# Attention values with queries on the partitions, and f32 loads cast on GpSimd, in a fused sliding-window attention and gated-convolution FFN

## The chip, the core and the metric

The kernel runs on one core of a Trainium2 chip. The metric is the device time of one execution in microseconds (us), the median of several runs. Runs of one kernel agree within 1.5% here.

Engine names as the profile writes them: PE is TensorE (matmuls), PEld its weight load, DVE is VectorE, ACT is ScalarE, POOL is GpSimd, SP is SyncE (here only an issuer of transfers). "SPq" and "POOLq" are their sequencers. A line number such as L237 is a line of that kernel's own file, so the same statement has different numbers in different kernels.

## The reference, cut to what matters

```python
def _attn_ref(q, k, v):                     # q, k, v: (8, 8, 576, 64) f32
    scores = np.matmul(q, k.transpose(0, 1, 3, 2)) / np.sqrt(64)
    mask = np.abs(pos[:, None] - pos[None, :]) <= 32      # sliding window, symmetric
    scores = np.where(mask, scores, -1e9)
    attn = np.exp(scores - scores.max(-1, keepdims=True))
    attn = attn / (attn.sum(-1, keepdims=True) + 1e-09)
    return np.matmul(attn, v)

def _moe_ref(x, w_in, conv_w, w_out):       # x: (8, 576, 512), w_in: 512x1024, w_out: 1024x512
    h = np.maximum(x @ w_in, 0.0)
    conv_out = sum(conv_w[k] * shifted(h, k) for k in range(3))   # along the sequence
    gate = 1.0 / (1.0 + np.exp(-conv_out))
    return h * gate @ w_out                 # f32, (8, 576, 512)
```

Eight batches go through attention (eight heads, handled as four pairs) and then through the FFN. All matmuls of the kernels read bf16 and write f32 tiles.

## The kernel before

Each batch's q, k and v are loaded by transfers that GpSimd issues. They cast f32 to bf16 on the way. A row of one head is 256 bytes in HBM, so every transfer is made of 256-byte pieces. The loads of batch 0 are issued head by head (32 issues), those of later batches block by block:

```python
    def load_qk(b, per_head):
        i = b % NLD
        for (dst, src) in ((qnb_pp[i], q), (knb_pp[i], k)):
            if not per_head:
                _load_rows(nc, nc.gpsimd, dst, src, b, 0, H, S)        # 5 transfers, all heads
        if per_head:
            for h in range(H):
                _load_rows(nc, nc.gpsimd, qnb_pp[i], q, b, h, 1, S)    # 2 transfers for one head
                _load_rows(nc, nc.gpsimd, knb_pp[i], k, b, h, 1, S)
    # ... load_v: blocks of v on gpsimd into ve; then vo, the same rows shifted by 64, copied from ve:
        nc.sync.dma_start(vo[0:64, :, :, :], ve[64:128, 0:NBLK - 1, :, :])
        nc.sync.dma_start(vo[64:128, :, :, :], ve[0:64, 1:NBLK, :, :])
```

GpSimd also makes the diagonal matrices of the convolution weights, in its queue ahead of the loads of batch 1, and VectorE scales w_out by 0.5 once it has landed:

```python
    def load_weights():
        # ... w_in on gpsimd, conv_w on sync
        for kk in range(3):
            for m in range(MB):
                nc.gpsimd.tensor_scalar(
                    out=diag_w[:, kk, m, :], in0=ident,
                    scalar1=conv_w_sb[:, kk, m:m + 1], scalar2=None, op0=ALU.mult,
                )
    def load_w_out():
        nc.gpsimd.dma_start(w_out_sb, moe_w_out.rearrange("(c p) f -> p c f", p=128))
        nc.vector.tensor_scalar(out=w_out_sb, in0=w_out_sb, scalar1=0.5, ..., op0=ALU.mult)
```

Attention for a pair of heads: q and k are transposed on TensorE, the scores come out key-major (keys on the partitions), are exponentiated and masked, and then the values are computed **transposed** (head dimension on the partitions, queries along the free axis), which is the form the FFN wants. The sums of the softmax come from a matmul with a matrix of ones, so each sum is repeated on 64 partitions, and the reciprocal is taken of all 128x576 copies:

```python
    def job_av(g):
        # ...
        for t in range(NT):
            for e in range(2):
                nc.tensor.matmul(flat(po)[64*e:64*e+64, 64*t:64*t+64], vt[:, 2*pr+e, :],
                                 attn[:, e, 64*t:64*t+64], start=True, stop=True)
        for (x0, x1) in ((0, 512), (512, S)):
            for e in range(2):
                nc.tensor.matmul(flat(pd)[64*e:64*e+64, x0:x1], ones, attn[:, e, x0:x1],
                                 start=True, stop=True)
        rec = apool.tile([128, S], FP32, name="rec", tag="rec")
        nc.vector.reciprocal(rec, flat(pd)[:, 0:S])
        nc.vector.tensor_tensor(out=xT[b][:, pr, :], in0=flat(po)[:, 0:S], in1=rec, op=ALU.mult)
```

The FFN's jobs (`job_ph`: w_in and ReLU; `job_pc`: convolution, tanh and gate; `job_py`: w_out and store) of one batch are interleaved with the attention jobs of the next.

The softmax here doesn't subtract the row's maximum and nothing guards it: scores larger than these inputs give would overflow.

## Time and profile before

| | before |
|---|---|
| time, median | 348.03 us (347.66 to 349.21), 3 runs |
| profiled span | 345.0 us |
| start, until the last `xT` of batch 0 is written | 73.9 us |
| seven periods, one batch each | 237.8 us, 34.0 each |
| tail (last FFN alone) | 33.3 us |

The page of the profile, cut: busy time by engine; the span in 40 slices of 8.6 us (a digit is the busy tenths; PEclk is the clock granted to TensorE in tenths); the chain of waits that ended last, by engine and by line.

```profile
PE 254.0 (74%) x2766; PEld 166.1 (48%) x2784; DVE 232.4 (67%) x215; ACT 155.9 (45%) x245; POOL 137.8 (40%) x187
...
PE   0024106558889888988898889998898889988995
...
POOL 8999999659350805080408140632200000000000
PEclk9999555559999999999999998999999999999999
...
PE 42%; DVE 25%; POOL 16%; ACT 10%; DMA 4%; issue 2%; POOLq 0%
...
L237 DVE RECIPROCAL rec<-ps 128x576 f32<-128x576 f32 x32 | 120.2, 3755 | 24.8 <-PE ps L228 24.8
```

No engine is full on average, and the chain is shared: that is the picture of engines that wait for one another in turn. The last line says that 32 reciprocals took 3,755 ns each, 120 us in all, half of all that VectorE did. The slices say where PE is empty or slack: the first nine, in which POOL is mostly full. In slices 5 to 9 the granted clock is about half. The runs speak against the clock as a cause of the long time: runs of this kernel with a mean granted clock of 0.92 or 0.93 took 346.7 to 350.4 us, those with 0.97 to 0.99 took 345.6 to 349.8.

How the start is spent shows in the chain in order of time (start us, duration us, what):

```profile
22.59 0.18 POOL ident masks.py:197
...
31.31 14.64 POOL diag_w L148 x24
45.96 4.26 POOL qnb_74 L28 x5
...
58.97 12.94 DMA w_out_sb<-in_moe_w_out_dram
71.92 1.23 DVE w_out_sb L155
73.15 0.68 DVE xT L238
73.87 3.28 PE ps L249 x13
```

Until 22.6 us POOL issues loads, and only then makes `ident`, which PE's first transpose waits for. POOL makes `diag_w` until 46 us, and only then issues the q and k of batch 1. Then the chain runs through the load of w_out and its scaling, which stands ahead of the last `xT` in VectorE's program. Three FFN matmuls (L249) already ran at 64.9 us and the others had to wait for that `xT`; from 73.9 us the FFN runs on.

The busy time by stretch, for the start, the seven periods and the tail (columns: from:to, length, then busy us and count of instructions for PE, PEld, DVE, ACT and POOL, then the granted clock, DMA share and GB/s):

```profile
0.00:73.90 73.90, 18.83 (x270) 13.52 (x271) 30.01 (x43) 12.93 (x20) 66.31 (x100) 0.73 1.14 99
73.90:311.70 237.80, 206.12 (x2322) 135.37 (x2337) 195.69 (x165) 128.03 (x204) 71.46 (x88) 0.98 0.83 87
```

In the periods PE is busy 87% and VectorE 82%; neither is full.

### The profile page before, as it was taken

The numbers are of one execution on the slowest core, as the hardware profiler recorded it, in microseconds if no ns is written. First come the engines' busy times: TensorE is split into PE (matmuls) and PEld (weight loads), VectorE is DVE, ScalarE is ACT, GpSimd is POOL, SyncE is SP. The second block draws the span as 40 slices with busy tenths as digits, with TensorE's granted clock in tenths as the row PEclk, the third lists the DMA queues.
The fourth block names the chain that finished last, engine by engine and source line by source line (L and its number), as shares of the span: only waits on it lengthen the run. The fifth ranks groups of instructions, "written<-read, shape, count | busy, mean of one in ns | idle before, by whom it ended". The sixth has DMA issues, their size and how long they took to land.

```text
span 345.0 us, 6548 instructions
## 1 busy us (share of the span) xinstructions
PE 254.0 (74%) x2766; PEld 166.1 (48%) x2784; DVE 232.4 (67%) x215; ACT 155.9 (45%) x245; POOL 137.8 (40%) x187
## 2 busy tenths in 40 slices
PE   0024106558889888988898889998898889988995
PEld 0024103336655655565556555655555655555652
DVE  3018333939997869787878696878786978793130
ACT  1015002225654645465546454556554655443552
POOL 8999999659350805080408140632200000000000
PEclk9999555559999999999999998999999999999999
DMA  8869689999948994999499939691911001100114
GB/s 41 54 43 118 136 55 132 169 162 135 145 31 101 128 132 30 104 123 137 58 103 117 145 25 107 90 171 38 120 68 63 2 2 61 61 33 2 62 63 153
DMA packets 123934, 30.33 MB, mean 88 GB/s; under 512 B 116736, under 2 KB 117760, under 8 KB 123904
## 3 DMA queue, kind: packets, MB, share of 16 engines
q0 software_dynamic: 114608, 16.26, 70.4%
q1 hardware_dynamic: 9296, 13.65, 12.7%
q8 instruction: 22, 0.36, 0.4%
q14 instruction: 8, 0.07, 0.1%
HBM read 32.52 MB, written 9.44 MB: 122 GB/s over the span
## 4 chain that ended last, share of the span: by engine, by line
PE 42%; DVE 25%; POOL 16%; ACT 10%; DMA 4%; issue 2%; POOLq 0%
DVE rec L237 17%; PE ps L290 16%; PE ps L249 13%; PE ps L266 9%; POOL diag_w L148 4%; DMA w_out_sb<-in_moe_w_out_dram 4%; ACT y_sb L297 3%; DVE gT L276 3%; ACT attn L205 2%; DVE xT L238 2%; POOL qnb_73 L20 2%; POOL knb_75 L20 2%; ACT tn L273 2%; DVE attn L206 2%; PE ps L220 2%
## 5 line engine op out<-in xcount | busy, mean ns | idle before, releaser
L237 DVE RECIPROCAL rec<-ps 128x576 f32<-128x576 f32 x32 | 120.2, 3755 | 24.8 <-PE ps L228 24.8
L249 PE MATMUL ps<-xT,w_in_sb 128*128 128x288 bf16 x512 | 77.3, 293 | 20.8 <-DVE xT L238 11.4
L249 PEld LDWEIGHTS <-w_in_sb 128*128 128x128 bf16 x512 | 50.4, 99 | 38.7 <-issue 24.8
L290 PE MATMUL ps<-w_out_sb,gT 128*128 128x512 bf16 x270 | 64.3, 379 | 2.0 <-ACT tn L273 0.6
L273 ACT ACTIVATE tn<-ps 128x576 f32<-128x576 f32 x64 | 41.8, 653 | 25.1 <-PE ps L266 23.5
L266 PEld LDWEIGHTS <-diag_w 128*128 128x128 bf16 x384 | 35.0, 97 | 20.2 <-issue 11.4
L205 ACT ACTIVATE attn<-ps 128x576 bf16<-128x576 f32 x64 | 38.6, 652 | 11.2 <-PE ps L196 11.2
L290 PEld LDWEIGHTS <-gT 128*128 128x128 bf16 x288 | 27.7, 98 | 32.7 <-issue 2.2
L297 ACT COPY y_sb<-ps 128x1024 f32<-128x1024 f32 (+1 forms) x20 | 18.5, 927 | 53.2 <-PE ps L290 53.2
L185 ACT CAST qT<-ps 128x576 bf16<-128x576 f32 x32 | 20.4, 636 | 47.6 <-PE ps L176 47.6
L206 DVE TENSOR_TENSOR attn<-attn,mask 128x1152 bf16<-128x1152 bf16 x32 | 24.0, 750 | 22.4 <-ACT attn L205 22.4
L276 DVE SCALAR_TENSOR_TENSOR gT<-tn,hT_85 128x576 bf16<-128x576 f32 x32 | 23.6, 738 | 15.6 <-ACT tn L273 15.2
L255 ACT ACTIVATE hT_84<-ps 128x576 bf16<-128x576 f32 x32 | 20.9, 655 | 25.9 <-PE ps L249 25.5
L104 POOL DMA_DIRECT2D ve_78<-in_v_dram x24 | 18.9, 830 | 33.6 <-PE ps L220 33.6
L266 PE MATMUL ps<-hT_85,diag_w 128*128 128x288 bf16 x192 | 28.5, 286 | 3.1 <-ACT hT_85 L255 2.9
L255 ACT ACTIVATE hT_85<-ps 128x576 bf16<-128x576 f32 x32 | 20.8, 654 | 22.0 <-PE ps L249 21.8
L266 PE MATMUL ps<-hT_84,diag_w 128*128 128x288 bf16 x192 | 28.7, 288 | 2.4 <-ACT hT_84 L255 2.4
L104 POOL DMA_DIRECT2D ve_77<-in_v_dram x24 | 19.0, 831 | 23.6 <-PE ps L220 22.5
L238 DVE TENSOR_TENSOR xT<-ps,rec 128x576 bf16<-128x576 f32 x32 | 23.9, 747 | 5.9 <-PE ps L220 5.8
L28 POOL DMA_DIRECT2D qnb_74<-in_q_dram x20 | 16.9, 864 | 20.5 <-PE ps L176 20.3
L176 PE MATMUL ps<-ident,qnb_73 128*128 128x128 bf16 (+1 forms) x80 | 7.3, 228 | 24.1 <-POOL ident masks.py:199 23.9
L276 DVE SCALAR_TENSOR_TENSOR gT<-tn,hT_84 128x576 bf16<-128x576 f32 x32 | 23.2, 731 | 2.5 <-ACT tn L273 2.5
(68 smaller groups left out, 276.2 us busy)
## 6 DMA issues: line engine op xcount, KB each, us to landing
out_dram<-y_sb SPq DMA_DIRECT2D x16, 512.0 KB, 3.3
vo_79<-ve_77 SPq DMA_DIRECT2D x8, 256.0 KB, 4.7
qnb_74<-in_q_dram POOLq DMA_DIRECT2D x16, 128.0 KB, 5.9
knb_76<-in_k_dram POOLq DMA_DIRECT2D x16, 128.0 KB, 6.2
vo_80<-ve_78 SPq DMA_DIRECT2D x8, 256.0 KB, 4.1
ve_77<-in_v_dram POOLq DMA_DIRECT2D x12, 128.0 KB, 4.5
ve_78<-in_v_dram POOLq DMA_DIRECT2D x12, 128.0 KB, 4.3
qnb_73<-in_q_dram POOLq DMA_DIRECT2D x12, 128.0 KB, 7.4
```

Source lines behind the costliest of these rows:

```text
L104: nc.gpsimd.dma_start(ve[d0:d0 + s1 - s0, c, :, :], v[b, :, s0:s1, :].rearrange("h p d -> p h d"),)
L205: nc.scalar.activation(attn[:, e, :], flat(pss[e])[:, 0:S], AF.Exp, bias=0.0, scale=scale)
L206: nc.vector.tensor_tensor(out=attn, in0=attn, in1=mask.rearrange("p t x -> p (t x)")[:, None, :].broadcast_to([128, 2, S]), op=ALU.mult,)
L237: nc.vector.reciprocal(rec, flat(pd)[:, 0:S])
L238: nc.vector.tensor_tensor(out=xT[b][:, pr, :], in0=flat(po)[:, 0:S], in1=rec, op=ALU.mult)
L249: nc.tensor.matmul(ps[:, gg, 0:TG], w_in_sb[:, kc, m * 128:(m + 1) * 128], xT[b][:, kc, gg * TG:(gg + 1) * TG], start=(kc == 0), stop=(kc ...
L255: nc.scalar.activation(hT[:, m, 1:S + 1].rearrange("p (gg x) -> p gg x", x=TG), ps[:, :, 0:TG], AF.Relu)
L266: nc.tensor.matmul(ps[:, gg, 0:TG], diag_w[:, kk, m, :], hT[:, m, gg * TG + kk:gg * TG + kk + TG], start=(kk == 0), stop=(kk == 2),)
L273: nc.scalar.activation(tn.rearrange("p (gg x) -> p gg x", x=TG), ps[:, :, 0:TG], AF.Tanh, bias=0.0, scale=0.5)
L276: nc.vector.scalar_tensor_tensor(out=gT[b // 2][:, m, b % 2, :], in0=tn, scalar=1.0, in1=hT[:, m, 1:S + 1], op0=ALU.add, op1=ALU.mult,)
L290: nc.tensor.matmul(ps[:, i, :], g_[:, m, 128 * tb:128 * tb + 128], w_out_sb[:, m, :], start=(m == 0), stop=(m == MB - 1),)
L297: nc.scalar.copy(out=y_sb[:, 0:n, :], in_=ps[:, 0:n, :])
```

## The change

Its intent is in two halves.

**The attention half.** The value matmuls get attention as the stationary operand and v, with a 65th column of ones, as the moving one. So the result is query-major: queries on the partitions, and the softmax sum as one more column. The reciprocal is taken of 128x10 sums instead of 128x576. The price: the result must be transposed on TensorE (`job_xt`) and copied from PSUM by VectorE.

**The load half.** q, k and v are loaded as f32, without a cast, on SyncE's queue (the profile lists it as "hardware_dynamic"; here: the hardware queue) into staging tiles; GpSimd casts them (23 casts of 512 columns a batch). `vo` is cast from the staging tile instead of copied by a transfer. The loads and casts are spread between the jobs. Batch 0 is loaded in 15 blocks. `ident` comes early, `diag_w` moves from GpSimd to VectorE, and the scaling of w_out disappears (the 0.5 goes into the ReLU).

The core of the diff (cuts marked `# ...`; the load order, the merge of the streams and the moved memsets are left out):

```diff
-    ve_pp = [pp.tile([128, NBLK, H, 64], BF16, name=f"ve{i}") for i in range(NLD)]
+    qst = pp.tile([128, NBLK, H, 64], FP32, name="qst")      # kst, vst alike
+    ve_pp = [pp.tile([128, NBLK, H, 65], BF16, name=f"ve{i}") for i in range(NLD)]
 # ...
+    def load_block(dst, src, b, c, lo):
+        s0, s1 = max(0, lo), min(S, lo + 128)
+        fixed(nc.sync.dma_start(
+            dst[s0 - lo:s1 - lo, c, :, :], src[b, :, s0:s1, :].rearrange("h p d -> p h d")))
+    def cast(out_, in_):
+        fixed(nc.gpsimd.tensor_scalar(
+            out=out_, in0=in_, scalar1=1.0, scalar2=0.0, op0=ALU.mult, op1=ALU.add))
 # ...
+    for t_ in ve_pp + vo_pp:
+        nc.vector.memset(t_[:, :, :, 64], 1.0)
 # ...  diag_w
-                nc.gpsimd.tensor_scalar(
+            nc.vector.tensor_scalar(
 # ...  load_w_out
-        nc.vector.tensor_scalar(
-            out=w_out_sb, in0=w_out_sb, scalar1=0.5, scalar2=None, op0=ALU.mult
-        )
 # ...  job_av
+        for c in range(NBLK):
             for e in range(2):
-                nc.tensor.matmul(
-                    flat(pd)[64 * e:64 * e + 64, x0:x1],
-                    ones,
-                    attn[:, e, x0:x1],
-                    start=True, stop=True,
-                )
+                for j in range(2):
+                    t = min(2 * c + j, NT - 1)
+                    nc.tensor.matmul(
+                        pf[64 * j:64 * j + 64, AVS * c + 65 * e:AVS * c + 65 * e + 65],
+                        attn[:, e, 64 * t:64 * t + 64],
+                        (ve if t % 2 == 0 else vo)[:, t // 2, 2 * pr + e, :],
+                        start=True, stop=True,
+                    )
-        rec = apool.tile([128, S], FP32, name="rec", tag="rec")
-        nc.vector.reciprocal(rec, flat(pd)[:, 0:S])
+        rec = apool.tile([128, NBLK, 2], FP32, name="rec", tag="rec")
+        nc.vector.reciprocal(rec, po[:, :, :, 64])
         nc.vector.tensor_tensor(
-            out=xT[b][:, pr, :], in0=flat(po)[:, 0:S], in1=rec, op=ALU.mult
+            out=xn[b][:, :, 2 * pr:2 * pr + 2, :], in0=po[:, :, :, 0:64],
+            in1=rec[:, :, :, None].broadcast_to([128, NBLK, 2, 64]), op=ALU.mult,
         )
+    def job_xt(g):
+        t_ = transpose_into(slot(), lambda c: xn[b][:, c, 2 * pr:2 * pr + 2, :]...)
+        nc.vector.tensor_copy(out=xT[b][:, pr, :], in_=t_)
 # ...  job_ph
+            bias=0.0, scale=0.5,
```

## The prediction

> **What bounds it now.** Span 345.0 us; PE is busy 74%, DVE 67% (busy table). The chain of waits is shared: PE 42%, DVE 25%, POOL 16%; its largest line is the reciprocal `rec` on DVE (17%). There are three stages.
>
> 1. Start, 0 to about 74 us. In the timeline, POOL issues 32 small loads until 22.3 us, so `ident` is late and PE starts at 23.85. Then POOL makes `diag_w` (31.2 to 46 us), so the loads of batch 1 start at 45.9 and PE waits for them at 49 to 55. DVE then sits on the `w_out_sb` scaling until 73.1, behind a load that took 12.9 us. The steady FFN begins at 73.9 us, at half clock until 80.
> 2. Seven periods of one batch each. The same `xT` copy on the chain recurs at 138.0, 172.9, 207.4, 243.8, 278.3 us: about 35 us a period. Summed from start-to-start times of the timeline, PE needs about 27 us a period. DVE needs 30 (four reciprocals of 3.76 us are 15 of it). Neither is full; they alternate.
> 3. Tail, about 312 to 345 us: PE alone, dense.
>
> **What the change does.**
> - DVE: a pair's reciprocal goes from 128x576 (3.76 us) to 128x10 (estimate 0.15-0.2). The multiply goes from 576 to 640 columns (0.75 to about 0.8), and a 128x576 PSUM copy (0.75, as `kT`) is added. That is 4.5 to about 1.8 us a pair, about 88 us in all: busy 232 to about 150, 19 us a period, no longer limiting.
> - PE: the `ones` matmuls go (about 1.1 us a period), and four sets of transposes come (0.3 us each); the AV matmuls take about as long. Still 27 to 28 us a period.
> - Loads: 1024 rows of 256 B each on the hardware queue, in f32, with no POOL issue (0.83-0.92 us each) and no `vo` transfers. The old queue moved about 1,000 to 1,200 rows/us; the hardware queue moved the 4-byte pieces of `conv_w` at over 1,300/us. A batch's 13,824 rows take 10 to 14 us, which does not limit.
> - POOL: 23 casts of 512 columns per batch. `diag_w` (128 columns) came every 0.58 us; I estimate 0.9 to 1.15 us for 512, so 21 to 26 us a period. [...] the two `diag_w` that met the mask multiply came after 1.12 and 0.85 us instead of 0.58. Twelve such DVE instructions a period (mask, `gT`) cost POOL up to 6 us more. So POOL lands at 27 to 32 us, level with PE: the new rival.
>
> **Time.** Start: q and k in by about 13 us, PE from about 15, first AV about 20, FFN from about 41 instead of 74: gain about 32 us. Periods: 35 to about 31 us, with PE above 85% busy: gain about 27 us. Tail unchanged. 348 - 59 = about **289 us**; 8 in 10 between 272 and 312. Faster by over 2%: 0.94; within 2%: 0.04; slower: 0.02.
>
> **What would show it.** PE's first matmul near 15 us; FFN matmuls from about 41 us; recurrence of `xT` at 29-32 us; DVE share near 50%; `rec` gone from the chain, which becomes mostly PE; casts at 0.9-1.15 us, some stretched to 1.5+ beside mask and `gT`.
>
> **What would make it wrong.** Casts above 1.3 us, or long blocking: POOL then sets the period (34 us or more, about 320 us), with PE transposes waiting for casts. [...] If PE packs as in the tail, 275.

Three statements are cut out of the recorded text, because no trace or run of this case shows what they said: a general statement on contention between VectorE and GpSimd (what was measured of it here stands near the end), one on loads behind stores, one on the lowest rate at which the start would hold. No term of the sum goes with them: 348 - 32 - 27 = 289 us, as recorded. Three terms were estimates, which the trace before did not show: the 0.15 to 0.2 us of the short reciprocal; what 384 more columns add to a GpSimd instruction, from the 0.58 us of `diag_w` to 0.9 to 1.15; and the contention, which extends two delays in that trace (1.12 and 0.85 us instead of 0.58, so 0.54 and 0.27 more) to twelve instructions a period, `gT`'s among them, whose effect it had not seen. The two rates are in the trace before: GpSimd issued the 4,608 rows of one q in 4.26 us, about 1,080 rows/us, and the 3,072 pieces of `conv_w` took 2.31 us from the first to the last, about 1,330 a us.

## More of the kernel before

The attention stream is ahead by two pairs: before the values of a batch's last pair, the program has the transposes of the first two pairs of the **next** batch.

PE's longest wait in total, after that for `ident` at the start, is the FFN's wait for values that VectorE has not delivered (total us, times, longest us):

```profile
PE ps L249 <- DVE xT L238: 11.4, 11, 3.5
```

## The result, and the profile after

| | before | after |
|---|---|---|
| time, median of the same rounds | 348.62 us (347.66 to 350.84) | 284.78 us (284.04 to 285.84) |
| ratio after/before | | 0.8164 (95%: 0.8114 to 0.8213) |
| profiled span | 345.0 us | 282.3 us |
| start | 73.9 us | 44.5 us |
| seven periods | 237.8 us (34.0 each) | 204.4 us (29.2 each) |
| tail | 33.3 us | 33.4 us |

Four runs of each. A ratio is the mean time of one kernel's runs over that of the other's of the same rounds, so it is not quite the ratio of the medians. The stages are cut, to about 0.1 us, at the end of the last `xT` copy of batch 0 and of batch 7. The gain is 29.4 us in the start and 33.4 us in the periods, together the 62.7 us by which the spans differ, to rounding.

The page of the changed kernel's profile, the same lines (slices of 7.1 us):

```profile
PE 247.8 (88%) x2880; PEld 169.4 (60%) x2880; DVE 164.0 (58%) x269; ACT 159.3 (56%) x253; POOL 130.4 (46%) x189
...
PE   0356649987899999999999999999999999999994
...
POOL 4583579996788358244756273736353000000000
PEclk9999999999999999999999999999999999999999
...
PE 75%; DMA 8%; ACT 7%; SPq 4%; DVE 2%; issue 1%; POOL 1%; ACTq 0%
```

The chain is now TensorE's: 75%, with VectorE down from 25% to 2% and GpSimd from 16% to 1%. PE is full from slice 12 on. By stretch:

```profile
0.00:44.50 44.50, 21.08 (x257) 14.54 (x258) 23.52 (x68) 16.36 (x26) 25.52 (x45) 1.00 1.22 194
44.50:248.90 204.40, 197.19 (x2442) 137.27 (x2442) 133.04 (x193) 127.35 (x206) 104.91 (x145) 1.00 0.71 143
```

In the periods PE is busy 96% of the time (28.2 of 29.2 us). Before it was 206.1 of 237.8. So of the 33.4 us that the periods lost, 24.5 us is PE's waiting and 8.9 us its busy time. The latter is not fewer matmuls: the run below that only shortens the reciprocal has all the matmuls of before, and from the first FFN matmul of batch 1 to that of batch 7 PE is busy 170.9 us in it, against 181.3 before and 171.8 after. The same matmuls follow each other more densely there. The wait for `xT` shown above has shrunk:

```profile
PE ps L251 <- DVE xT L241: 1.2, 1, 1.2
```

VectorE is busy 19.0 us a period (133.04/7) instead of 28.0, GpSimd 15.0 us.

The new short reciprocal, the multiply and the casts, each by the instructions that use one tile (min/median/max ns, first and last start):

```profile
L228 DVE RECIPROCAL rec<-ps x32: 207/221/222, 26.8 to 245.8; 128x10 f32<-128x10 f32 x32
L229 DVE TENSOR_TENSOR xn<-ps,rec x32: 810/824/825, 27.1 to 246.0; 128x640 bf16<-128x640 f32 x32
```

```profile
L79 POOL TENSOR_SCALAR qnb_76<-qst x20: 614/621/1207, 5.5 to 163.8; 128x512 bf16<-128x512 f32 x20
```

The start of the chain, in order of time:

```profile
0.80 0.43 SPq L74
...
4.43 2.01 SPq L74
...
12.14 5.02 DMA vst<-in_v_dram
17.23 0.61 POOL ve_80 L79
17.84 4.58 DMA qst<-in_q_dram
22.42 9.59 DMA kst<-in_k_dram
...
33.70 4.55 DMA kst<-in_k_dram
38.32 0.63 POOL knb_79 L79
```

It is a chain of loads. SyncE's issues of a load (L74), 0.43 us at first, soon take up to 2 us each (0.42 to 3.5 us over the 40 loads of q; the cause was not looked for); then the chain passes from one landing to the next until the cast of `knb_79` at 38.3 us. `knb_79` is the k of batch **1**: the program has the transposes of batch 1's first two pairs ahead of the last values of batch 0, so the q and k of two batches and the v of one, 23,040 rows (2 x 9,216 + 4,608), stand before the first FFN. How fast the rows come shows in PE's timeline, where the transposes of blocks of 1,024 rows, q and k in turn, follow the casts (start us, duration us, engine, operation, idle time before it and its releaser):

```profile
10.12 0.40 PE L165 MATMUL ps<-ident,knb_78 128*128 128x128 bf16 x2 [0.79 <-POOL knb_78 L79]
11.33 0.40 PE L165 MATMUL ps<-ident,qnb_76 128*128 128x128 bf16 x2 [0.81 <-POOL qnb_76 L79]
12.53 0.39 PE L165 MATMUL ps<-ident,knb_78 128*128 128x128 bf16 x2 [0.81 <-POOL knb_78 L79]
```

A block every 1.2 us is 1,024/1.2, about 850 rows/us. At that rate 23,040 rows take 27 us, an estimate from these lines; waits for casts and the loads of the weights come on top.

### The profile page after: what moved, and what is told of

It reads as the page before. It is cut to its first block, busy times and chain, and to the rows that moved or that the text cites. A ratio compares the mean times of both kernels' runs of the same rounds, so it can differ in the third digit from the quotient of the medians.

```text
span 282.3 us, 6977 instructions
## 1 busy us (share of the span) xinstructions
PE 247.8 (88%) x2880; PEld 169.4 (60%) x2880; DVE 164.0 (58%) x269; ACT 159.3 (56%) x253; POOL 130.4 (46%) x189
## 4 chain that ended last, share of the span: by engine, by line
PE 75%; DMA 8%; ACT 7%; SPq 4%; DVE 2%; issue 1%; POOL 1%; ACTq 0%
PE ps L251 23%; PE ps L293 22%; PE ps L269 17%; PE ps L165 6%; DMA kst<-in_k_dram 5%; ACT y_sb L300 5%; SPq L74 4%; PE ps L216 3%; PE ps L190 3%; DMA vst<-in_v_dram 2%; DMA qst<-in_q_dram 2%; ACT tn L276 1%; ACT hT_87 L257 1%; DVE gT L279 1%; ACT attn L199 1%
## 5 line engine op out<-in xcount | busy, mean ns | idle before, releaser
L251 PE MATMUL ps<-xT,w_in_sb 128*128 128x288 bf16 x512 | 75.4, 291 | 3.1 <-DVE xT L241 1.2
L251 PEld LDWEIGHTS <-w_in_sb 128*128 128x128 bf16 x512 | 47.5, 99 | 16.7 <-issue 3.6
L200 DVE TENSOR_TENSOR attn<-attn,mask 128x1152 bf16<-128x1152 bf16 x32 | 25.9, 810 | 23.7 <-ACT attn L199 23.6
L279 DVE SCALAR_TENSOR_TENSOR gT<-tn,hT_88 128x576 bf16<-128x576 f32 x32 | 26.5, 831 | 19.0 <-ACT tn L276 18.8
L279 DVE SCALAR_TENSOR_TENSOR gT<-tn,hT_87 128x576 bf16<-128x576 f32 x32 | 28.0, 878 | 5.3 <-ACT tn L276 5.2
L229 DVE TENSOR_TENSOR xn<-ps,rec 128x640 bf16<-128x640 f32 x32 | 26.3, 822 | 0.8
L241 DVE CAST xT<-ps 128x576 bf16<-128x576 f32 x32 | 23.7, 751 | 4.4 <-PE ps L165 4.4
L79 POOL TENSOR_SCALAR vo_83<-vst 64x512 bf16<-64x512 f32 x32 | 23.9, 748 | 2.4
L79 POOL TENSOR_SCALAR knb_79<-kst 128x512 bf16<-128x512 f32 x20 | 13.7, 684 | 22.5 <-DMA kst<-in_k_dram 17.9
L216 PEld LDWEIGHTS <-attn 128*64 128x64 bf16 x640 | 14.6, 115 | 11.8 <-issue 9.5
L79 POOL TENSOR_SCALAR ve_81<-vst 128x512 bf16<-128x512 f32 x20 | 14.0, 700 | 16.6 <-DMA vst<-in_v_dram 8.4
```

The costliest lines, as they stand in the source:

```text
L79: fixed(nc.gpsimd.tensor_scalar(out=out_, in0=in_, scalar1=1.0, scalar2=0.0, op0=ALU.mult, op1=ALU.add))
L200: nc.vector.tensor_tensor(out=attn, in0=attn, in1=mask.rearrange("p t x -> p (t x)")[:, None, :].broadcast_to([128, 2, S]), op=ALU.mult,)
L229: nc.vector.tensor_tensor(out=xn[b][:, :, 2 * pr:2 * pr + 2, :], in0=po[:, :, :, 0:64], in1=rec[:, :, :, None].broadcast_to([128, NBLK, 2, ...
L241: nc.vector.tensor_copy(out=xT[b][:, pr, :], in_=t_)
L251: nc.tensor.matmul(ps[:, gg, 0:TG], w_in_sb[:, kc, m * 128:(m + 1) * 128], xT[b][:, kc, gg * TG:(gg + 1) * TG], start=(kc == 0), stop=(kc ...
L279: nc.vector.scalar_tensor_tensor(out=gT[b // 2][:, m, b % 2, :], in0=tn, scalar=1.0, in1=hT[:, m, 1:S + 1], op0=ALU.add, op1=ALU.mult,)
```

## The experiments

The theory to be tested: the two halves of the change act on different stages. The attention half shortens the periods because VectorE's long reciprocal made PE wait, and leaves PE as the limit. The load half shortens the start. Rivals: that the casts on GpSimd set the new period; that the matmuls saved, not the reciprocal, gave the gain; that the hardware queue, or the spreading, is what shortened the start.

For every run the trace also gives two numbers that separate the stages. "Front" is when the first FFN matmul of batch 1 starts. "Rest" is from there to the start of the last matmul of that line, of batch 7. What follows, to the end of the span, is 14.6 or 14.7 us in every one of these kernels. Both are read from the profiled run, so they don't sum exactly to the medians. The before of each row's ratio ran on the same chip in the same rounds (medians 348.06 to 348.84 us).

| kernel | median us | ratio (95%) | front us | rest us |
|---|---|---|---|---|
| before | 348.62 | 1 | 101.4 | 229.0 |
| after | 284.78 | 0.8164 (0.8114 to 0.8213) | 72.1 | 195.6 |
| attention half alone | 302.55 | 0.8693 (0.8665 to 0.8721) | 91.3 | 194.6 |
| load half alone | 330.46 | 0.9497 (0.9460 to 0.9534) | 81.3 | 229.9 |
| before, reciprocal shortened | 300.98 | 0.8642 (0.8611 to 0.8673) | 90.2 | 194.2 |
| after, q and k cast twice | 289.46 | 0.8319 (0.8283 to 0.8356) | 75.8 | 196.9 |
| after, all cast twice | 334.88 | 0.9627 (0.9585 to 0.9669) | 84.9 | 233.7 |
| after, no transposes of the values | 273.32 | 0.7847 (0.7824 to 0.7871) | 68.1 | 188.7 |
| after, loads on the casting queue | 278.25 | 0.7987 (0.7948 to 0.8026) | 67.9 | 194.6 |
| after, q and k in 1,536-byte pieces | 279.62 | 0.8036 (0.7997 to 0.8075) | 65.6 | 197.9 |
| that on the casting queue, v direct | 294.94 | 0.8450 (0.8390 to 0.8509) | 77.5 | 201.6 |
| attention half, front cleared | 294.78 | 0.8466 (0.8417 to 0.8515) | 83.7 | 194.6 |
| that, and batch 0 in blocks | 281.86 | 0.8110 (0.8064 to 0.8155) | 69.5 | 194.6 |
| 1,536-byte pieces, v early | 281.24 | 0.8083 (0.8036 to 0.8129) | 67.7 | 196.1 |

### One half alone

The kernel before with only the new `job_av` and `job_xt`, the 65-column `ve` and `vo`, and the order of the jobs that goes with it; loads, `diag_w` and the w_out scaling as before.

```diff
 # the kernel before, with
+        nc.vector.reciprocal(rec, po[:, :, :, 64])          # 128x10, query-major
+    def job_xt(g): ...
 # and load_qk, load_v, load_weights, load_w_out unchanged but for "0:64" in ve's destination
```

> The kernel before with the query-major attention values alone (65th column, short reciprocal, transposes); its loads stay as they were. My theory (the two halves of the change act in different stages: this half shortens the periods, the loads shorten the start): periods from 34.0 to 29-30 us, FFN still starting late at 66 to 74 us, in all 305 to 318 us. Rival (the periods were held up by the pooled loads, and the new attention only moves work from DVE to PE): 335 us or more.

It came to 302.55 us, 45.8 below the before of the same rounds (348.34) and a little better than expected, with a correct answer. Rest is 194.6 us, as in the whole change (195.6). So the periods belong to the attention half, all of them. Front falls by 10 us too; it holds the first period as well.

The changed kernel with the old `job_av` (ones matmuls, long reciprocal, no transposes):

```diff
 # the changed kernel, with
-        nc.vector.reciprocal(rec, po[:, :, :, 64])
+        nc.vector.reciprocal(rec, flat(pd)[:, 0:S])         # 128x576, as before
-    def job_xt(g): ...
```

> The changed kernel with the old key-major attention values (ones matmuls, 128x576 reciprocal); loads, casts and diag_w as in the change. My theory: FFN starts at 44 to 50 us instead of 74, the periods stay at 34 to 36 us because DVE needs 30 us of each, in all 318 to 330 us. Rival (casts on GpSimd get in the way of DVE, which now has little room, and eat the gain): periods of 37 us or more, in all 340 or more.

It came to 330.46 us, 17.9 below before, just past the top of what was expected, with a correct answer. Rest is 229.9 us: nothing of the periods was gained. Its chain of waits by engine, and by line (cut by the view itself):

```profile
DVE 43%; PE 37%; ACT 12%; SPq 3%; issue 2%; DMA 1%; POOL 0%
DVE rec L231 27%; PE ps L286 12%; PE ps L244 11%; PE ps L262 7%; DVE gT L272 7%; ACT attn L199 5%; DVE xT L232 3%; DVE attn L200 3%; PE ps L190 3%; SPq L75 3%; ACT y_sb L293 2%; ACT hT L250 2%; ACT tn L269 2%; DVE kT L183 2%; PE ps L214 2%
```

With the start cleared the reciprocal's share of the chain rises to 27%. The two gains, 45.8 and 17.9, sum to 63.7 us; the whole change gained 63.8. The halves are additive.

### Is it the reciprocal, or the matmuls?

The kernel before, untouched but for the width of the reciprocal; the multiply reads a constant tile with the 128x10 result in it. The answer is wrong (relative error 0.096).

```diff
-        nc.vector.reciprocal(rec, flat(pd)[:, 0:S])
+        nc.vector.reciprocal(rec_pp[g % 3][:, 0:10], flat(pd)[:, 0:10])
+        rec = rec_pp[g % 3]
```

> The kernel before, with the reciprocal cut to 10 of its 576 columns and nothing else moved (wrong result on purpose; the multiply reads a constant tile). My theory (the reciprocal's time on DVE is all that the attention half gains, and the transposes cost nothing net because the ones matmuls go): about as e1, within 4 us, so 303 to 318 us. Rival (the query-major layout itself helps PE, or its transposes cost): this differs from e1 by 8 us or more.

It came to 300.98 us, against 302.55 for the real attention half, with rest 194.2 against 194.6. The gain of the attention half is VectorE's reciprocal time. On TensorE the change is about even: from the first FFN matmul of batch 1 to that of batch 7 PE is busy 170.9 us in both runs, so the transposes cost what the ones matmuls had cost.

### Does TensorE set the new period?

The changed kernel without the transposes of the values; VectorE copies the untransposed tile into `xT` (two copies instead of one). Its output is wrong, which doesn't matter for the time.

```diff
     def job_xt(g):
-        t_ = transpose_into(slot(), lambda c: xn[b][:, c, ...])
-        nc.vector.tensor_copy(out=xT[b][:, pr, :], in_=t_)
+        nc.vector.tensor_copy(out=xT[b][:, pr, 0:512].rearrange(...), in_=xn[b][:, 0:4, ...])
+        nc.vector.tensor_copy(out=xT[b][:, pr, 512:S], in_=xn[b][:, 4, 2 * pr, :])
```

> The changed kernel without the transposes of the attention output (wrong result on purpose; DVE copies xn to xT instead). If PE's own work sets the period, taking away 4 x 0.30 us a period returns about that: 272 to 278 us against 284.8. If the period is set by waits between the engines or by another engine, it stays within 1%, 282 or more.

It came to 273.32 us, 11.5 us below the change, or 0.36 us for each of the 32 pairs. Between the first FFN matmuls of batches 1 and 7 PE's busy time fell by 6.2 us (171.8 to 165.6) and the time by 6.8 us (176.5 to 169.7), while VectorE did slightly more instructions (301 against 269). TensorE work taken away comes off the time whole, so TensorE sets the period. Where the 0.6 us beyond it comes from was not tried.

### How far is GpSimd from being the limit?

The changed kernel with each q and k cast of batches 1 to 7 done twice (10 more casts a batch), and with every cast of these batches done twice (23 more).

```diff
+        def cast_n(out_, in_):
+            for _ in range(2 if b > 0 else 1):
+                cast(out_, in_)
 # e5: q and k use cast_n;  e5b: ve and vo use it as well
```

> The changed kernel with every cast of q and k done twice from batch 1 on (right result). My theory now (a cast takes about 0.7 us, so GpSimd has slack in a period): GpSimd work a period goes from about 16 to 23 us, still under PE's 29, so the time stays within 1%, 282 to 288 us. Rival (the prediction's figure: GpSimd is level with PE): each period grows by 5 us or more, in all 310 us or more.

It came to 289.46 us, 1.6% above the change. The later periods did not move (28.4 to 30.5 us, in the change 28.4 to 30.4), though GpSimd rose from 46% to 63% busy. The loss is in the start (the first FFN matmul 2.3 us later) and the first two periods (29.9 and 31.5 us instead of 28.5 and 30.4).

> The changed kernel with all casts done twice from batch 1 on (right result). GpSimd work a period then is about 46 x 0.72 = 33 us, above PE's 29.2: GpSimd should set the period at 33 to 36 us while it has casts to do, in all 300 to 320 us. If time stays under 290, GpSimd's casts overlap each other more than their spacing tells.

It came to 334.88 us, beyond the range expected: some four fifths of the change's gain are gone. Six of the seven periods are 34.6 to 42.2 us, and between 55 and 280 us GpSimd was busy 204.2 of 225 us. The chain by engine, then what PE waited for (total us, times, longest us):

```profile
POOL 42%; PE 37%; DMA 7%; SPq 5%; issue 3%; ACT 2%; DVE 2%; POOLq 0%
```

```profile
PE ps L169 <- POOL qnb L79: 30.0, 19, 6.2
PE ps L220 <- POOL vo L79: 11.9, 7, 3.8
```

Now GpSimd is the limit, and the wait for a cast is the sign. Two things follow. The prediction's rival exists, but at about twice the casts that the change has: the ten extra casts of the first run fitted, 23 extra did not. And when GpSimd did become the limit, the period was longer than its own work (204.2 of 225 us). Over the whole run GpSimd waited 6.7 us for loads of q and 2.9 us for loads of k. Already in the change SyncE's issues of loads wait for casts of the staging tiles (for the casts of `qnb_77` ten times, 9.0 us in all, 2.2 at most). Whether later casts held the loads up further here was not shown: the chain has 7% DMA and 5% SPq, the change's 8% and 4%. The granted clock was also lower in this run (0.92 on average from 55 to 280 us); PE was busy only 187.0 of these 225 us, and what the clock adds was not separated.

### What of the load half gives its gain?

The changed kernel with its order, blocks, spreading, `ident`, `diag_w` and ReLU scale kept, but with q, k and v loaded on GpSimd's casting queue as before, and `vo` copied by transfers. No staging tiles, no casts. (`ident` is made ahead of the loads, as these are now issued by GpSimd.)

```diff
-        fixed(nc.sync.dma_start(
-            dst[s0 - lo:s1 - lo, c, :, :], src[b, :, s0:s1, :].rearrange("h p d -> p h d")
+        fixed(nc.gpsimd.dma_start(
+            dst[s0 - lo:s1 - lo, c, :, 0:64], src[b, :, s0:s1, :].rearrange("h p d -> p h d")
-                half(vo[0:64, c, :, 0:64], vst[64:128, c, :, :])
+                fixed(nc.sync.dma_start(vo[0:64, c, :, :], ve[64:128, c, :, :]))
```

> The changed kernel with its loads put back on the software queue (casting to bf16 as they go, vo halves copied by SBUF transfers), but in the changed kernel's order and places: ident first, diag_w on DVE, no w_out scaling, loads spread between the jobs. Theory A (the start got shorter because nothing else is in front of the loads any more, not by the hardware queue itself): FFN starts at 40 to 48 us, in all 280 to 292. Theory B (the hardware queue is what makes the start short): FFN starts at 55 us or later, in all 295 or more.

It came to 278.25 us with a correct answer: the fastest kernel, 6.5 us faster than the change in medians, with intervals of the ratio that do not touch (0.8026 at most against 0.8114 at least). So moving the loads to the hardware queue, with casts on GpSimd, is not where the gain comes from; as a whole it costs. In the profiled spans (277.1 against 282.3) the 5.2 us lie in the first FFN matmul (41.6 against 43.6 us), the first period (26.2 against 28.5) and the second (29.4 against 30.4); the later ones are equal. For these 256-byte rows, with the f32 writes and the casts that the hardware queue brought here, the hardware queue was the slower way: 284.78 against 278.25 us. The two kinds of queue in the two profiles (packets, MB, share of 16 engines), the change first:

```profile
q1 hardware_dynamic: 117440, 37.76, 67.1%
```

```profile
q0 software_dynamic: 114128, 16.26, 101.1%
```

The share sums the packets' times. For about as many packets the casting queue moves 16 MB, in bf16; the other 38 MB, of which 9.4 MB are stores. PE's timeline of this run, with the transposes straight behind the landings, tells part of the reason:

```profile
8.45 0.39 PE L153 MATMUL ps<-ident,knb 128*128 128x128 bf16 x2 [0.49 <-DMA knb<-in_k_dram]
9.34 0.40 PE L153 MATMUL ps<-ident,qnb 128*128 128x128 bf16 x2 [0.49 <-DMA qnb<-in_q_dram]
```

A block came every 0.89 us here, about 1,150 rows/us, against 1.2 us in the change, where each of these casts (0.62 us) first waited 0.58 us for its landing. So in this stretch the landings, not the casts, set the slower pace; the tenth and last q or k block of batch 0 was transposed at 14.3 us against 17.0. Whether the landings are faster by the queue or by the smaller writes is not separated.

What, then, was the gain of the load half? The next two runs built it up from the other side: the attention half alone (302.55 us) with the old loads, and first only the front cleared, that is `ident` first, `diag_w` on VectorE with conv_w loaded earlier for it, no w_out scaling:

```diff
+    make_identity(nc, ident)
     load_qk(0, True)
 # diag_w: nc.gpsimd.tensor_scalar -> nc.vector.tensor_scalar; w_out scaling out, scale=0.5 in the ReLU
```

> e1 (new attention values, old loads in their old places and order, per-head first loads) with only the front of the program cleared: ident made before the loads are issued, diag_w built on DVE instead of GpSimd, w_out not scaled. Theory (the start was long because GpSimd did 15 us of diag_w and made ident late, not because the loads were not spread between the jobs): most of the 24 us between e1 and e7 comes back, 276 to 286 us. Rival (spreading the loads and their finer blocks are what counts): 292 us or more.

It came to 294.78 us, a much smaller gain than expected: 7.8 of the 24 us between 302.55 and 278.25. Its chain still begins with the 32 issues of batch 0's q and k, until 22.5 us, with the v of batch 0 and w_in behind them:

```profile
21.71 0.77 POOL knb L20
23.03 0.74 POOL mask L131
25.07 4.04 POOL ve L104 x5
29.11 2.14 POOL w_in_sb L151 x4
31.25 2.40 POOL qnb L28 x3
```

So one word was changed: batch 0's q and k come in 10 block transfers instead of 32 per head.

```diff
-    load_qk(0, True)
+    load_qk(0, False)
```

> e10 with one word changed: q and k of batch 0 are loaded in 10 transfers of all heads (1,024 rows each) instead of 32 per-head ones. e10 left 16.5 us to e7, and its first v load was issued at 23.8 us against 10.0 in e7. Theory (the number of issues on GpSimd ahead of v and of batch 1 is the rest): 277 to 285 us. Rival (spreading the loads between the jobs is the rest): 290 us or more.

It came to 281.86 us: 12.9 us for the one word. The same stretch of its chain, with everything some 13 us earlier:

```profile
6.05 4.19 POOL knb L28 x5
10.24 0.74 POOL mask L131
11.50 0.73 POOL mask L135
12.24 4.06 POOL ve L104 x5
```

This kernel has the old queue, no casts and unspread loads, and it is as fast as the whole change (0.8110 against 0.8164, the intervals just overlap). So the load half's gain over the attention half alone is: fewer issues on GpSimd ahead of the later loads, most of it, and a cleared front. (The two were tried in this order only; in the other order their shares could differ.) Spreading the loads between the jobs, with the finer `vo` copies and the issue order that go with it, is worth the last step to 278.25.

### Are the rows too short?

The changed kernel with q and k loaded as 1,536-byte pieces (six successive rows of a head on one partition), on the hardware queue. The transposes then read every sixth row, and the copies to `qT` and `kT` put them back in order.

```diff
+    QR = 6                                    # rows per partition
+            src[b, 2*pr:2*pr+2, :, :].rearrange("h (p c) d -> p h c d", c=QR)
-            nc.scalar.copy(out=qT, in_=t_)
+            nc.scalar.copy(out=qT.rearrange("p (x c) -> p x c", c=QR), in_=t_)
```

> The changed kernel with q and k loaded as six neighbouring rows per partition (pieces of 1,536 B instead of 256 B, one transfer per head pair) and transposed as six blocks of 96; order of loads otherwise the same. If the start waits for the transfers' rate (about 205 GB/s of 256 B pieces for the first 44 us), it shortens by 5 to 12 us: 273 to 280 us. If the start is set by the chain through the engines, or the strided read of PSUM costs in each period, 282 us or more.

It came to 279.62 us, correct: 5 us faster than the change. Front is the shortest of all (65.6 us), and the transfers of the first 44 us move at 225 GB/s instead of 194 (the trace's figure for the change; the expectation put it at about 205). So the loads of the change do limit its start. This run also loads pair by pair instead of block by block, and the order was not separated from the longer pieces. But part of the gain is given back in the second period (32.0 us against 30.4).

Its chain in the start no longer runs through q and k, but through the small load of conv_w (9.5 us) and `diag_w` on VectorE until 19.2 us. So in a further run `diag_w` was spread between the jobs, v was loaded after the first two pairs of q and k, and w_in was issued later:

```diff
+        first = 2 if b == 0 else NP
+        for pr in range(first): yield from pair(pr)
+        yield from vs()
 # diag_w as jobs merged into the first period; vo of batch 0 cast on gpsimd instead of on ACT
```

> e8 (hardware queue, 1,536 B pieces of q and k) with what its chain of waits named in the start taken away: diag_w on DVE behind the first attention jobs instead of before them, v of batch 0 loaded after two head pairs, vo casts of batch 0 on GpSimd instead of ScalarE, w_in issued after batch 0's casts. If the start was held by these, batch 1's FFN begins 4 to 10 us earlier than in e8: 269 to 276 us. If the loads' rate holds it, within 2 us of e8's 279.6. If the result is wrong, the spread diag_w (which e9 shares) is the suspect for e9's wrong result; if right, the 64x96 transposes or the vo loads of e9 are.

It came to 281.24 us, no gain over 279.62. The expected rival was right in the number. The chain shows what fills the start instead of loads: the casts of `ve` and `vo` on GpSimd from 10 to 19.4 us, then `diag_w` on VectorE among the attention's own work. It also gives a second width of cast:

```profile
18.75 0.62 POOL L88 TENSOR_SCALAR vo<-vst 64x512 bf16<-64x512 f32 x1
19.45 0.83 POOL L88 TENSOR_SCALAR qnb<-qst 96x768 bf16<-96x768 f32 x1
```

From 512 to 768 columns a cast grows by 0.21 us, 0.8 ns a column.

The last variant put the long pieces on the casting queue and loaded both `ve` and `vo` from HBM, so v was read twice:

```diff
-        fixed(nc.sync.dma_start(              # q, k pairs and v blocks
+        fixed(nc.gpsimd.dma_start(
+                vs.append((lambda c=c: load_block(vo, v, b, c, 128 * c + PAD), lambda: None))
```

> A version meant to beat both: e7's software-queue loads, with q and k as pieces of 1,536 B per partition (one transfer per head pair, transposed per head as 12 blocks of 64x96), vo loaded from the input instead of copied, v of batch 0 ahead of its last head pairs, diag_w on DVE spread over the first period behind the first attention jobs. If the start is what is left to gain: batch 1's FFN begins 6 to 12 us earlier than in e7 and the periods stay at 29 to 30 us, 266 to 274 us. If twelve small transposes a job cost PE more than five large ones, the periods grow by 0.5 to 1.5 us and the gain is lost: 276 us or more.

It came to 294.94 us, and its answer is wrong (relative error 0.200), not on purpose. Its time is therefore weak evidence. Its chain in the first 72 us is mostly the v loads (one `vo` load took 8.1 us and one 12.2 us). The cause of the wrong answer was not found; the suspects are the transposes of 96 rows by 64 columns, the direct `vo` loads and the long pieces on the casting queue, which no correct variant has.

## Why the prediction was right or wrong

Right: 289 us was predicted, within 272 to 312, and 284.8 us measured. Point by point:

| step of the prediction | predicted | measured |
|---|---|---|
| start of the FFN | 74 to ~41 us, gain ~32 | 73.9 to 44.5 us, gain 29.4 |
| period | 35 to ~31 us, gain ~27 | 34.0 to 29.2 us, gain 33.4 |
| tail | unchanged | 33.3 and 33.4 us |
| reciprocal 128x10 | 0.15 to 0.2 us | 0.22 us |
| multiply, 640 columns | ~0.8 us | 0.82 us |
| VectorE a period | 19 us | 19.0 us |
| VectorE in all | ~150 us, near 50% | 164.0 us, 58% |
| PE a period | 27 to 28 us | 28.2 us busy |
| casts | 0.9 to 1.15 us, some 1.5+ | 0.62 us median, at most 1.24 |
| GpSimd a period | 27 to 32 us | 15.0 us |
| a batch's rows | 10 to 14 us, "does not limit" | ~16 us (estimate at 850 rows/us), and it limited the start |

**Right: the mechanism.** The long reciprocal (3.76 us for 128x576, where the multiply of the same shape took 0.75) made PE wait; shortened, it is out of the chain, which became mostly PE's (75%), and PE's wait for `xT` fell from 11.4 to 1.2 us. The short-reciprocal run shows that this is the cause, and the run without transposes that PE is the new limit.

**Wrong: "So POOL lands at 27 to 32 us, level with PE: the new rival."** The estimate took `diag_w`, 0.59 us for 128 columns on GpSimd, and added for the fourfold width; how much, was the author's estimate and not shown by the trace. The cast of 512 columns took 0.62 us, and one of 768 (on 96 partitions) took 0.83. By the 0.8 ns a column between these two, 128 columns of a cast would take about 0.3 us (an estimate from these two), so by this estimate `diag_w` was slow for something other than its width: it reads bf16, and its scalar comes from a tile instead of being a constant. What of this matters was not tried. The step that failed is the transfer of a duration from one form of an instruction to another. With 15.0 us a period GpSimd is in the chain with 1%, and this is the likely reason why the period came out below the prediction: PE could pack to 96%, where the prediction had allowed for two engines in step. Doubling the casts showed both that there is room (q and k alone: no later period moves) and where it ends (all: 334.88 us). It also shows some luck. Over the first six periods GpSimd was busy 17.6 us each in the change, 25.2 with q and k cast twice (289.46 us in all) and 34.4 with all cast twice (334.88 us). The predicted 27 to 32 us lie between the last two, so with casts as dear as it assumed its 289 us would have been at risk.

**Half right: the contention.** In the trace of the change the mask multiply grew from a mean of 0.75 to 0.81 us, the gate multiply from 0.73 and 0.74 to 0.83 and 0.88 us (by its two input tiles), and casts stretched beside them: the 101 casts that met no mask or gate multiply took 0.61 to 0.64 us, the 75 that met one took 0.85 us on average and 1.24 at most. In the run on the casting queue, without casts, the gate multiply took 0.76 us. But at this size it does not limit anything here: VectorE has 2% of the chain and GpSimd 1%.

**Wrong in part: the loads.** "A batch's 13,824 rows take 10 to 14 us, which does not limit" held for the periods and not for the start. Two errors: the rate was taken from other transfers (the casting queue's rows, about 1,080 a us, and 4-byte pieces, about 1,330 a us), and was in fact about 850 rows/us on the hardware queue (the casting queue did reach 1,150 in the run on it); and the rows counted were those of one batch, where the program needs the q and k of two before its first FFN. "PE's first matmul near 15 us" was also off: it came at 6.18 us, as the transposes run block by block behind the loads. But the early start brought the first values no earlier than predicted: they came at 21.4 us (predicted: about 20).

**Not asked by the prediction: which part of the load half helps.** It counted the hardware queue and the missing issues together. The runs separate them: the issues and the cleared front give the gain, and the hardware queue with its casts takes back some 6 us. The two main errors (casts too dear by 45% or more, loads too cheap) have opposite signs and partly cancel in the 289 us.

## What to carry to other kernels

When two engines alternate and neither is full, look for one long instruction that the other waits for: shortening VectorE's 3.76 us reciprocal 32 times gave 46 us, while the extra transposes that made it possible were paid by matmuls that went away (302.55 us with the transposes, 300.98 with the old matmuls and the short reciprocal). In a start-up, count the issues that stand ahead of what the first full-speed stage needs, on the queue that issues them, for all batches that the program order demands; replacing 32 small transfers by 10 was worth 13 us. And before moving loads to another queue with casts on an engine, try the old queue in the new order: here that was the fastest version, correct, at 278.25 us.
